# Packed attention and two float32 MLPs on one core: seven small-tile groups a batch in place of twelve, and the first output weights kept as one float32 part until the second stage

## The chip, the core and the metric

The kernel runs on one core of one Trainium2 chip. The core has five engines that run side by side, each through its own list of instructions in order: TensorE (PE in the profile, with its weight loads as PEld), VectorE (DVE), ScalarE (ACT), GpSimd (POOL) and SyncE (SP), which here issues every DMA. They wait for each other by semaphores. The metric is the device time of one execution in microseconds (us), and lower is better.

## The reference

Eight batches of eight heads with 576 tokens are attended in two steps (32 packing queries over all keys, then all queries over the 32 packed rows). The result goes through two MLPs. All inputs are float32, and the weights come to the kernel as float64 words.

```python
def sm_attn(qq, kk, vv):
    s = scale * np.matmul(qq, kk.transpose(0, 1, 3, 2))
    s = s - np.max(s, axis=-1, keepdims=True)
    a = np.exp(s)
    a = a / (np.sum(a, axis=-1, keepdims=True) + 1e-09)
    return np.matmul(a, vv)
p_packed = sm_attn(p, k, v)
out = sm_attn(q, p_packed, p_packed)
x = out.transpose(0, 2, 1, 3).reshape(8 * 576, 512)
h = x @ w_in;  x = np.maximum(0.01 * h, h) @ w_out               # first MLP, 512 -> 2048 -> 512
h = x @ w_in2; return (h * (1 / (1 + np.exp(-1.702 * h)))) @ w_out2
```

## The kernel before

The program has four stages, one after the other. TensorE is fed in all of them with float32 numbers split in a high part (`fp32r`) and a low rest, so that one product is three matmuls (high by high, high by low, low by high).

**Stage 1, attention and the first half of the first MLP** (about the first 354 us). It runs over the batches `b`; each batch has 32 steps `n`, and each step is one call of `l1`: six matmuls of 128x288 into one of three PSUM banks, and a leaky ReLU on ACT (L343), which writes a tile `g`. Four steps fill one `g` tile, which goes to DRAM by SP. After step `n` of batch `b` the agenda is played for step `32*b + n`: `at(step, ...)` puts work there, and `pieces(piece, steps)` spreads the parts of a generator over steps. So the table of step numbers in the middle of the function sets the order on every engine. What is spread is the attention of batch `b+1`: `s1` (scores of the packing queries, softmax numerators `e`), `packed` (transposes `t` of `e`, the product `pp` with the values, its transpose, the packed rows `ppk`), `s2` for two halves of the tokens (scores, softmax, the split `a`), and `prod_m` for four quarters `c` of the hidden units (`ppk` by `w1`, split in `m`). Quarter `c` of `m` is needed from step `8*c` on. `s1`, `pp`, `s2` and `prod_m` are float32 matmuls on parts of the array, 64x32 or 128x32 each, called small-tile groups here; they stand between runs of `l1` matmuls. They write PSUM tiles with the tag `aux`, of which there are five.

Beside it stand the weights of the output product. `combine` takes a 128x512 piece of `w_out1` (sixteen in all), makes float32 of the float64 words (ACT L121 and L122, DVE L125 and L128, POOL L129), forms seven Strassen-like combinations on DVE, splits them in a high and a low part (ACT L155, DVE L157) and stores both in DRAM (`wo1c`). The words are loaded 8 steps before their use.

**Stage 2** computes `y = g w_out1` with a seven-product scheme in six blocks of 768 tokens. A product has 8 steps of six matmuls of 128x384 each (L660). `high` (ACT L496) and `split` (DVE L107) prepare the moving operand a few steps ahead, and `weights` loads the combination `COMBO[p]` in two pieces a product: both parts for `wo1`, one float32 part for `wo2`, which is split by `half` on ACT and DVE. The first five pieces (`EARLY`) are loaded in stage 1, the other nine in the first block of stage 2. **Stage 3** is the first half of the second MLP, **stage 4** its second half, which uses the same `weights`, `prepare` and `evacuate` as stage 2, with `wo2`.

In the diff, `px` is a pool of SBUF that lives until step 24 of the last batch; at that point the loads of the first raw operands of stage 2 (`br`, twelve DMAs) are issued by SP.

Of the kernel before, what the change touches and what calls it, by code (L numbers as in the profile page):

```python
# [46 lines left out]
def packed_attention_moe_moe_kernel(tc, qT, kT, vm, vt, pT, w_in1, w_out1, w_in2, w_out2, out):  # L47
# [8 lines left out]
    wi2c, wo2c = (tc.dram_tile([NJ, P, 7, 256], F32, name=f"{n}_scratch") for n in ("wi2", "wo2"))  # L56
    wo1c = tc.dram_tile([NJ, P, 2, 7, 256], F32, name="wo1_scratch")
# [22 lines left out]
    with ExitStack() as ctx:  # L80
# [51 lines left out]
        def combine(name, source, scratch):  # L132


            conv = pools["conv"]
# [5 lines left out]
            b = conv.tile([P, 8, P], F32, tag="b", name=f"b_{name}")  # L141
            v = conv.tile([P, 4 * P], F32, tag="v", name=f"v_{name}")
# [6 lines left out]
            if scratch is not wo1c:  # L149
                yield  # L150
                nc.sync.dma_start(place(name, scratch), b[:, 1:8])
# [57 lines left out]
        def after(load, b):  # L209
            if b < B:  # L210
                load(b)
# [39 lines left out]
        def packed(b):  # L251

            e, r = e1.pop(b)
            et = px.tile([P, 2, 5, P], F32, tag="et", name=f"et_{b}")
            rest = aux(f"tr_{b}")
            for par in range(2):
                t = aux(f"t1_{b}_{par}")
                for k in range(4):
                    nc.tensor.transpose(t[:, P * k:P * k + P], e[:, par, P * k:P * k + P], ident)
                nc.tensor.transpose(rest[:64, P * par:P * par + P], e[:, par, 512:576], ident)  # L260
                yield
                nc.scalar.copy(et[:, par, 0:4, :], t.rearrange("p (k n) -> p k n", k=4))
# [3 lines left out]
            o = px.tile([P, 2, D], F32, tag="o", name=f"o_{b}")  # L266
            for par in range(2):
                t = aux(f"pp_{b}_{par}")
                for k in range(5):
                    n = P if k < 4 else 64  # L270
                    for i in range(4):
                        c0 = D * (2 * (i % 2) + par)
                        nc.tensor.matmul(t[32 * i:32 * i + 32, :D], lhsT=et[:n, par, k, 32 * i:32 * i + 32],
                                         rhs=v[:n, i // 2, k, c0:c0 + D], start=(k == 0), stop=(k == 4))
                if par and b:
                    after(load_v, b + 1)
                yield
                nc.vector.tensor_scalar(o[:, par, :], t[:, :D], r[:, par:par + 1], None, op0=ALU.mult)
# [114 lines left out]
        run(pk, 4)  # L393
# [22 lines left out]
        for b in range(B):  # L416
            s = 32 * b
            if b + 1 < B:
                if b == 0:
                    first, second = (3, 4, 5, 5, 6, 7), (9, 9, 10, 10, 11, 12, 12, 13)  # L420
                    third, fourth = range(14, 22), range(16, 24)
                else:
                    first, second = (-3, -2, -2, 0, 1, 2), range(5, 13)
                    third, fourth = ([k + i for k in (0, 1, 2, 4, 5, 7, 10, 11)] for i in (13, 17))
                for piece, when in ((s1(b + 1), first), (packed(b + 1), second), (s2(b + 1, 0), third),
                                    (s2(b + 1, 1), fourth), (prod_m(b + 1, 0), range(26, 30))):
                    pieces(piece, [s + k for k in when])
            if b:
                for c in range(1, 4):
                    pieces(prod_m(b, c), [s + 8 * c - 6 + k for k in range(4)])  # L430
# [7 lines left out]
        def weights(first, halves, i, fq, home, scratch, nm):  # L438
# [17 lines left out]
            if scratch is wo1c:  # L456
                return
# [365 lines left out]
```

## Time and the profile before

| what | value |
|---|---|
| time, median of 3 runs (lowest, highest) | 1442.76 us (1441.86, 1443.36) |
| span of the profiled execution | 1443.2 us; no other time stands beside it |
| instructions | 26603 |
| PE busy, PEld busy | 97%, 91% of the span |
| DVE, ACT, POOL busy | 76%, 54%, 7% of the span |
| mean granted TensorE clock | 0.987 of full speed |
| DMA | 317.36 MB, mean 220 GB/s |

The profiled execution has no time of its own beside its span, and the span lies within the three runs, so that sums made against the span hold for the median with 0.4 us taken off. A busy PE is not a PE at its peak: where it stands between two kinds of work, or runs at the lower clock, it is still shown as busy. So the starts of its runs of matmuls, one after another, are read in the timeline.

### The profile page before, as it was taken

Reading aid. Unit: us, or ns where it says so; the run is one execution under the profiler, and the core shown is the slowest. Engines: PE = TensorE matmul, PEld = TensorE weight load, DVE = VectorE, ACT = ScalarE, POOL = GpSimd, SP = SyncE. Lnnn points to the kernel's source line nnn. Section 1 sums busy time; section 2 is a strip of 40 time slices with the busy share of each in tenths; the row PEclk is TensorE's granted clock in tenths of the full one; section 3 lists DMA queues with packets and bytes.
Section 4 is the critical chain, followed back from the end, with each engine's and each line's share of the span. In section 5 each row is a group of like instructions: output and inputs, shape, how many; then the busy total and the mean of one; then the engine's idle time right before and its main releaser. Section 6 shows DMA issues by size and latency. Waiting matters only on the chain. (4 is left out here: it accounts for less than half of the span.)

```text
span 1443.2 us, 26603 instructions
## 1 busy us (share of the span) xinstructions
PE 1395.0 (97%) x10400; PEld 1317.6 (91%) x10400; DVE 1089.9 (76%) x1690; ACT 784.8 (54%) x1413; POOL 95.4 (7%) x71
## 2 busy tenths in 40 slices
PE   5899999999999999999999999999999999999998
PEld 3577777778999999999999999999999999999998
DVE  5757777761879989888978788887559877677775
ACT  4656666665445545554566666666546444444443
POOL 2301011000001111110000001000000000000000
PEclk7999999999999999999999999999999999999999
DMA  9669998969985674664367868777667443515421
GB/s 357 215 231 335 314 318 289 335 211 336 355 295 163 219 242 123 218 219 133 119 219 252 276 231 273 236 259 248 214 231 239 168 142 121 176 56 165 152 68 45
DMA packets 228765, 317.36 MB, mean 220 GB/s; under 512 B 12576, under 2 KB 188704, under 8 KB 228640
## 3 DMA queue, kind: packets, MB, share of 16 engines
q1 hardware_dynamic: 228640, 315.67, 65.8%
q8 instruction: 81, 1.33, 0.4%
q14 instruction: 44, 0.36, 0.1%
HBM read 191.89 MB, written 123.73 MB: 219 GB/s over the span
## 5 line engine op out<-in xcount | busy, mean ns | idle before, releaser
L694 PE MATMUL h<-ya,wj 128*128 128x384 f32 x2016 | 356.3, 338 | 3.7 <-DVE ya L107 2.2
L694 PEld LDWEIGHTS h<-ya,wj 128*128 128x128 f32 x2016 | 353.2, 189 | 6.7 <-DVE ya L107 3.0
L338 PEld LDWEIGHTS h<-a,m 128*128 128x128 f32 x1536 | 211.7, 191 | 57.1 <-ACT g L343 27.0
L338 PE MATMUL h<-a,m 128*128 128x288 f32 x1536 | 234.9, 305 | 13.8 <-ACT a L315 6.5
L496 ACT CAST da<-dr 128x768 fp32r<-128x768 f32 x168 | 140.2, 836 | 171.3 <-PE sum L773 155.1
L773 PE MATMUL sum<-wo,da 128*128 128x256 f32 x1944 | 230.4, 280 | 0.0
L660 PE MATMUL y<-ba,wo 128*128 128x384 f32 x1296 | 227.7, 336 | 2.2 <-DVE ba L107 2.2
L773 PEld LDWEIGHTS sum<-wo,da 128*128 128x128 f32 x1944 | 229.8, 188 | 0.0
L660 PEld LDWEIGHTS y<-ba,wo 128*128 128x128 f32 x1296 | 224.5, 188 | 4.5 <-DVE ba L107 4.5
L496 ACT CAST ba<-br 128x768 fp32r<-128x768 f32 x168 | 140.6, 837 | 156.7 <-PE y L660 127.5
L107 DVE TENSOR_TENSOR da<-dr,da 128x768 fp32r<-128x768 f32 x168 | 160.5, 956 | 75.4 <-ACT da L496 74.4
L107 DVE TENSOR_TENSOR ba<-br,ba 128x768 fp32r<-128x768 f32 x168 | 172.2, 1028 | 41.6 <-ACT ba L496 41.4
L343 ACT ACTIVATE g<-h 128x288 f32<-128x288 f32 x256 | 105.2, 417 | 96.0 <-PE h L338 93.9
L773 PE MATMUL sum<-wo_early,da 128*128 128x256 f32 x1080 | 132.1, 285 | 2.4 <-ACT da L496 1.9
L773 PEld LDWEIGHTS sum<-wo_early,da 128*128 128x128 f32 x1080 | 131.2, 192 | 2.9 <-ACT da L496 2.2
L660 PE MATMUL y<-ba,wo_early 128*128 128x384 f32 x720 | 129.4, 340 | 3.7 <-ACT ba L496 2.7
L660 PEld LDWEIGHTS y<-ba,wo_early 128*128 128x128 f32 x720 | 125.7, 190 | 6.7 <-DVE ba L107 3.4
L327 DVE TENSOR_TENSOR m<-m,m 128x512 fp32r<-128x512 f32 x64 | 43.0, 683 | 49.8 <-ACT m L325 49.3
L129 POOL TENSOR_TENSOR b_wo<-v_wo,b_wo 128x512 int32<-128x512 int32 x32 | 42.3, 1322 | 519.9 <-DVE v_wo L128 414.9
L687 ACT ACTIVATE g<-cc 128x384 f32<-128x384 f32 x96 | 50.3, 524 | 30.8 <-DVE cc L710 26.3
L107 DVE TENSOR_TENSOR wj<-wjs,wj 128x512 fp32r<-128x512 f32 x92 | 58.0, 644 | 9.5 <-ACT wj L634 9.5
L702 DVE TENSOR_TENSOR uv<-uv,h 128x384 f32<-128x384 f32 x48 | 26.5, 552 | 47.0 <-PE h L694 37.6
(115 smaller groups left out, 1336.7 us busy)
## 6 DMA issues: line engine op xcount, KB each, us to landing
g_scratch<-g SPq DMA_DIRECT2D x64, 576.0 KB, 5.3
br<-g_scratch SPq DMA_DIRECT2D x96, 384.0 KB, 6.6
g_scratch<-g SPq DMA_DIRECT2D x96, 384.0 KB, 5.2
dr<-g_scratch SPq DMA_DIRECT2D x96, 384.0 KB, 5.0
wjs<-wi_scratch SPq DMA_DIRECT2D x23, 896.0 KB, 5.7
wo_scratch<-hl_wo SPq DMA_DIRECT2D x32, 448.0 KB, 5.9
wo<-wo_scratch SPq DMA_DIRECT2D x27, 512.0 KB, 9.3
k<-in_kT_dram SPq DMA_DIRECT2D x16, 576.0 KB, 6.7
```

Source lines behind the costliest of these rows:

```text
L107: at(step + 1, lambda: nc.vector.tensor_sub(*rest))
L129: nc.gpsimd.tensor_tensor(d, v.bitcast(I32), d, op=ALU.add)
L327: nc.vector.tensor_sub(m[:, 1, par, :], t[par], m[:, 0, par, :].bitcast(F32))
L338: nc.tensor.matmul(t[:, :TH], lhsT=m[:, ws, par, o:o + P], rhs=a[:, xs, par, :], start=(k == 0), stop=(k == 5))
L343: nc.scalar.activation(g1t[g][:, f % 2, hf * TH:hf * TH + TH], t[:, :TH], AF.Prelu, alpha=0.01)
L496: nc.scalar.copy(t[:, 0], src)
L660: nc.tensor.matmul(acc[BANK[p]][:, c, :HB], lhsT=w[:, ws, P * c:P * c + P], rhs=x[:, xs, :], start=(p in OPENS and f + m == 0), stop=(f == ...
L687: nc.scalar.activation(g[f][:, HB * i:HB * i + HB], src, AF.Gelu_apprx_sigmoid)
L694: nc.tensor.matmul(b, lhsT=w[:, ws, c, P * kk:P * kk + P], rhs=x[:, xs, kk, :], start=(p in OPENS and kk + s == 0), stop=(kk + s == 3), sk ...
L702: nc.vector.tensor_add(v, v, b)
L773: nc.tensor.matmul(b, lhsT=x[:, xs, P * c:P * c + P], rhs=w[:, ws, :], start=(p in OPENS and f == 0 and m == 0 and c != 1), stop=(f == NJ ...
```

## The change

Four things are changed. First, `combine` no longer splits the combinations of `w_out1`: they are stored as one float32 part of half the size, and `weights` loads one part and splits it by `half`, in stage 1 for the five early pieces and in stage 2 for the other nine, as for `w_out2`. Second, the words of `w_out1` are loaded 14 steps ahead of their use, alternately into tiles of `conv` and of `px`. Third, `packed` issues its ten transposes together, and its products `pp` for both head parities together, into one PSUM tile. Fourth, the table of steps is another one: the second half of `packed`, and the quarters 1 and 2 of `prod_m`, start at the same step, so do the two halves of `s2`, and so do quarter 0 of the next batch and quarter 3 of this one.

```diff
-    wo1c = tc.dram_tile([NJ, P, 2, 7, 256], F32, name="wo1_scratch")
+    wi2c, wo1c, wo2c = (tc.dram_tile([NJ, P, 7, 256], F32, name=f"{n}_scratch") for n in ("wi2", "wo1", "wo2"))
...
-            conv = pools["conv"]
+            conv = pools["px" if "px" in pools and name.endswith("1") else "conv"]
...
-            h = pools["px"].tile([P, 2, 7, P], F32R, tag="hl", name=f"hl_{name}")
-            nc.scalar.copy(h[:, 0], b[:, 1:8])
-            yield
-            nc.vector.tensor_sub(h[:, 1], b[:, 1:8], h[:, 0].bitcast(F32))
-            yield
-            for x in range(2):
-                nc.sync.dma_start(place(name, scratch)[:, x], h[:, x].bitcast(F32))
+            yield
+            nc.sync.dma_start(place(name, scratch), b[:, 1:8])
...
+            t = [aux(f"t1_{b}_{par}") for par in range(2)]
             rest = aux(f"tr_{b}")
             for par in range(2):
-                t = aux(f"t1_{b}_{par}")
                 for k in range(4):
-                    nc.tensor.transpose(t[:, P * k:P * k + P], e[:, par, P * k:P * k + P], ident)
+                    nc.tensor.transpose(t[par][:, P * k:P * k + P], e[:, par, P * k:P * k + P], ident)
+            for par in range(2):
                 nc.tensor.transpose(rest[:64, P * par:P * par + P], e[:, par, 512:576], ident)
-                yield
-                nc.scalar.copy(et[:, par, 0:4, :], t.rearrange("p (k n) -> p k n", k=4))
+            yield
+            for par in range(2):
+                nc.scalar.copy(et[:, par, 0:4, :], t[par].rearrange("p (k n) -> p k n", k=4))
...
-            for par in range(2):
-                t = aux(f"pp_{b}_{par}")
+            t = aux(f"pp_{b}")
+            for par in range(2):
...
-                    first, second = (-3, -2, -2, 0, 1, 2), range(5, 13)
-                    third, fourth = ([k + i for k in (0, 1, 2, 4, 5, 7, 10, 11)] for i in (13, 17))
...
-                    pieces(prod_m(b, c), [s + 8 * c - 6 + k for k in range(4)])
-        combined("wo1", range(30, 30 + 16 * 11, 11), 8)
...
+                first, second = range(-5, 1), (1, 2, 4, 5, 6, 7)
+                third, fourth, fifth = (9, 10, 11, 12, 13, 14, 16, 17), (9, 10, 12, 13, 16, 20, 22, 23), (15, 23, 24, 25)
...
+            for c, when in ((1, (4, 5, 6, 7)), (2, (4, 6, 7, 8)), (3, (15, 17, 18, 19))):
+                pieces(prod_m(b, c), [32 * b + k for k in when])
+        slots = [32 * b + k for b in range(1, B - 1) for k in (3, 18, 26) if k != 26 or b < 5]
...
-            if scratch is wo1c:
-                return
```

On PE, batch 3 (the first number behind a name is left out by the print, so `h_3_4_0` is batch 3, hidden block 4, token half 0, and `m_2_0` is quarter 2, parity 0) has before, from step 8 to step 12:

```order
L338 MATMUL h_3_4_0_2197<-a_3_0_1891,m_1_2134 128x288 x6
L273 MATMUL pp_0_2207<-v_1698,et_2159 32x64 x20
L338 MATMUL h_3_4_1_2232<-a_3_1_1948,m_1_2134 128x288 x6
L273 MATMUL pp_1_2241<-v_1698,et_2159 32x64 x20
L338 MATMUL h_3_5_0_2268<-a_3_0_1891,m_1_2134 128x288 x6
L218 MATMUL m_2_0_2277<-w_87,ppk_1750 32x512
L218 MATMUL m_2_1_2278<-w_87,ppk_1750 32x512
...
L338 MATMUL h_3_5_1_2289<-a_3_1_1948,m_1_2134 128x288 x6
L281 MATMUL t_4_2298<-ident,o_2206 128x128
L338 MATMUL h_3_6_0_2306<-a_3_0_1891,m_1_2134 128x288 x6
```

The changed program has, from step 4 to step 8 of the same batch (each kind of `m` row stands four times, alternating):

```order
L330 MATMUL h_3_2_0_2124<-a_3_0_1807,m_0_1938 128x288 x6
L264 MATMUL pp_2134<-v_1623,et_2086 32x64 x40
L207 MATMUL m_1_0_2180<-w_87,ppk_1690 32x512
L207 MATMUL m_1_1_2181<-w_87,ppk_1690 32x512
...
L207 MATMUL m_2_0_2190<-w_87,ppk_1690 32x512
L207 MATMUL m_2_1_2191<-w_87,ppk_1690 32x512
...
L330 MATMUL h_3_2_1_2205<-a_3_1_1900,m_0_1938 128x288 x6
L330 MATMUL h_3_3_0_2219<-a_3_0_1807,m_0_1938 128x288 x6
L273 MATMUL t_4_2227<-ident,o_2133 128x128
L330 MATMUL h_3_3_1_2233<-a_3_1_1900,m_0_1938 128x288 x6
L330 MATMUL h_3_4_0_2249<-a_3_0_1807,m_1_2215 128x288 x6
```

So four groups that had runs of `l1` between them now stand together, and quarter 1, first used by `h_3_4_0`, is made four steps before that use, where it had six.

On DVE, the low part of quarter 0 for batch 4 (`m_0_2556`) stands before behind these rows, ahead of the maxima of `s1` for batch 5:

```order
L308 TENSOR_TENSOR wf_1_2414<-wf_1_2414,s2s_1_2481 128x576
L317 TENSOR_TENSOR a_4_0_2455<-a_0_2454,a_4_0_2455 128x576
L313 STREAM_TRANSPOSE a_1_2510<-wf_1_2414 128x288 x2
...
L148 TENSOR_TENSOR b_wo_3_1_2441<-b_wo_3_1_2441 128x128
L157 TENSOR_TENSOR hl_wo_3_1_2544<-b_wo_3_1_2441,hl_wo_3_1_2544 128x896
L317 TENSOR_TENSOR a_4_1_2511<-a_1_2510,a_4_1_2511 128x576
L327 TENSOR_TENSOR m_0_2556<-m_0_0_2534,m_0_2556 128x512
L327 TENSOR_TENSOR m_0_2556<-m_0_1_2535,m_0_2556 128x512
L239 TENSOR_REDUCE mx_2615<-s_5_0_0_2582 128x1
```

In the changed program the same place reads:

```order
L127 SCALAR_TENSOR_TENSOR v_wo_3_1_2428<-v_wo_3_1_2428,raw_wo_3_1_2201 128x512
...
L144 TENSOR_TENSOR b_wo_3_1_2427<-b_wo_3_1_2427 128x128
L309 TENSOR_TENSOR a_4_1_2452<-a_1_2451,a_4_1_2452 128x576
L146 TENSOR_TENSOR b_wo_3_1_2427<-b_wo_3_1_2427 128x128
L147 TENSOR_TENSOR b_wo_3_1_2427<-b_wo_3_1_2427 128x128
L319 TENSOR_TENSOR m_0_2490<-m_0_0_2371,m_0_2490 128x512
L319 TENSOR_TENSOR m_0_2490<-m_0_1_2372,m_0_2490 128x512
L124 TENSOR_SCALAR raw_wo_4_0_2332<-raw_wo_4_0_2332 128x512
L228 TENSOR_REDUCE mx_2571<-s_5_0_0_2536 128x1
```

The 128x896 row `hl_wo` is gone from DVE, and most of the work of `s2` for batch 4 (`wf`, `a`) has moved up, away from quarter 0.

## Rows read from the trace of the kernel before

**Rows 1.** The page, part 1: busy time, share of the span, instructions.

```profile
PE 1395.0 (97%) x10400; PEld 1317.6 (91%) x10400; DVE 1089.9 (76%) x1690; ACT 784.8 (54%) x1413; POOL 95.4 (7%) x71
```

**Rows 2.** Windows cut at the starts of `s1`: length, busy by engine, clock, DMA share, GB/s.

```profile
85.99:124.06 38.07, 37.34 (x412) 29.94 (x411) 24.84 (x56) 24.47 (x62) 2.56 (x2) 1.00 0.88 293
...
244.69:283.49 38.80, 37.88 (x413) 30.10 (x412) 28.46 (x64) 26.82 (x65) 4.23 (x3) 1.00 0.99 327
283.49:319.80 36.31, 34.31 (x378) 27.43 (x377) 25.32 (x56) 23.92 (x59) 2.58 (x2) 1.00 0.68 217
```

**Rows 3.** Timeline of PE, one batch of stage 1: start, length, work, count.

```profile
85.99 1.20 PE L218 MATMUL s<-k,p 64*32 64x288 f32 x32
87.12 4.27 PE L338 MATMUL h<-a,m 128*128 128x288 f32 x30
91.32 1.09 PE L218 MATMUL m<-w,ppk 64*32 64x512 f32 x16
92.34 2.66 PE L338 MATMUL h<-a,m 128*128 128x288 f32 x18
94.83 0.60 PE L259 MATMUL t<-ident,e 128*128 128x128 f32 x4
...
95.30 1.04 PE L338 MATMUL h<-a,m 128*128 128x288 f32 x6
...
98.41 0.90 PE L273 MATMUL pp<-v,et 128*32 128x64 f32 x40
99.23 1.06 PE L338 MATMUL h<-a,m 128*128 128x288 f32 x6
100.22 0.90 PE L273 MATMUL pp<-v,et 128*32 128x64 f32 x40
...
105.75 0.72 PE L218 MATMUL s<-q,ppk 64*32 64x288 f32 x16
106.39 3.45 PE L338 MATMUL h<-a,m 128*128 128x288 f32 x24
```

**Rows 4.** Timeline of PE at the longest stall of stage 1.

```profile
204.47 1.21 PE L218 MATMUL s<-k,p 64*32 64x288 f32 x14 [2.24 <-DVE m L327]
205.61 6.56 PE L338 MATMUL h<-a,m 128*128 128x288 f32 x30
```

**Rows 5.** Window just behind that stall, columns as in rows 2.

```profile
206.00:210.00 4.00, 4.00 (x18) 4.00 (x18) 2.29 (x7) 1.85 (x4) 0.00 (x0) 0.50 1.00 296
```

**Rows 6.** Groups of ACT and DVE, 85 to 320: busy, mean ns, idle before.

```profile
L343 ACT ACTIVATE g<-h 128x288 f32<-128x288 f32 x191 | 78.7, 417 | 68.2 <-PE h L338 66.2 <-DMA k<-in_kT_dram 1.0 <-DMA wo_scratch<-hl_wo 0.4
L325 ACT CAST m<-m 128x512 fp32r<-128x512 f32 x48 | 28.4, 592 | 0.0
L155 ACT CAST hl_wo<-b_wo 128x896 fp32r<-128x896 f32 x16 | 15.1, 945 | 8.9 <-DVE b_wo L148 8.6 <-issue 0.3
...
L327 DVE TENSOR_TENSOR m<-m,m 128x512 fp32r<-128x512 f32 x48 | 32.1, 682 | 26.2 <-ACT m L325 25.8
L157 DVE TENSOR_TENSOR hl_wo<-b_wo,hl_wo 128x896 fp32r<-128x896 f32 x16 | 17.3, 1080 | 6.7 <-ACT hl_wo L155 5.4 <-DMA raw_wo<-in_w_out_dram 1.1
```

**Rows 7.** Timeline of SP, ACT and PE where stage 2 starts.

```profile
348.83 10.84 SPq L473 DMA_DIRECT2D br<-g_scratch  x12
...
356.15 0.83 ACT L496 CAST ba<-br 128x768 fp32r<-128x768 f32 x1 [1.41 <-DMA br<-g_scratch]
...
357.04 0.44 PE L660 MATMUL y<-ba,wo_early 128*128 128x384 f32 x1 [2.74 <-ACT ba L496]
```

**Rows 8.** Groups of DVE, 1086 to 1138: the weight splits of stage 4.

```profile
L107 DVE TENSOR_TENSOR wo<-wo 128x512 fp32r<-128x512 f32 x18 | 12.0, 682 | 0.0
```

**Rows 9.** Window in the same block, columns as in rows 2.

```profile
1117.00:1127.00 10.00, 10.00 (x87) 10.00 (x87) 10.00 (x14) 7.45 (x12) 0.00 (x0) 1.00 0.59 173
```

**Rows 10.** Timeline of PE: two waits of `pp` in the first batch.

```profile
21.30 1.15 PE L273 MATMUL pp<-v,et 64*32 64x64 f32 x48 [1.99 <-DVE et L263]
...
61.37 0.32 PE L273 MATMUL pp<-v,et 64*32 64x64 f32 x8 [1.94 <-DVE et L263]
```

More of the change, by code (lines that the diff above doesn't have):

```diff
@@ L140, in combine @@
             yield
[L141 to L142 removed]
+            b = conv.tile([P, 8, P], F32, tag="cb", name=f"b_{name}")
+            v = conv.tile([P, 4 * P], F32, tag="cv", name=f"v_{name}")
             yield from to_f32(b[:, 0:4].rearrange("p i w -> p (i w)"), raw.rearrange("p i (w t) -> p (i w) t", t=2), v, True)
@@ L272, in packed @@
                         c0 = D * (2 * (i % 2) + par)
-                        nc.tensor.matmul(t[32 * i:32 * i + 32, :D], lhsT=et[:n, par, k, 32 * i:32 * i + 32],
+                        nc.tensor.matmul(t[32 * i:32 * i + 32, D * par:D * par + D], lhsT=et[:n, par, k, 32 * i:32 * i + 32],
                                          rhs=v[:n, i // 2, k, c0:c0 + D], start=(k == 0), stop=(k == 4))
[L275 to L278, printed above, removed]
+            if b:
+                after(load_v, b + 1)
+            yield
+            for par in range(2):
+                nc.vector.tensor_scalar(o[:, par, :], t[:, D * par:D * par + D], r[:, par:par + 1], None, op0=ALU.mult)
             yield
@@ L392, in packed_attention_moe_moe_kernel @@
         run(w1p[3], 2)
-        run(pk, 4)
+        run(pk, 2)
         run(w1p[4], 2)
@@ L415, in packed_attention_moe_moe_kernel @@
             pieces(prod_m(0, c), when)
-        for b in range(B):
+        for b in range(B - 1):
             s = 32 * b
[L418 to L422, printed above, removed]
-                    first, second = (-3, -2, -2, 0, 1, 2), range(5, 13)
-                    third, fourth = ([k + i for k in (0, 1, 2, 4, 5, 7, 10, 11)] for i in (13, 17))
[L425 to L429, printed above, removed]
-                    pieces(prod_m(b, c), [s + 8 * c - 6 + k for k in range(4)])
-        combined("wo1", range(30, 30 + 16 * 11, 11), 8)
+            if b == 0:
+                first, second = (3, 4, 5, 5, 6, 7), (9, 10, 11, 12, 13, 13)
+                third, fourth, fifth = range(14, 22), range(16, 24), range(26, 30)
+            else:
+                first, second = range(-5, 1), (1, 2, 4, 5, 6, 7)
+                third, fourth, fifth = (9, 10, 11, 12, 13, 14, 16, 17), (9, 10, 12, 13, 16, 20, 22, 23), (15, 23, 24, 25)
+            for piece, when in ((s1(b + 1), first), (packed(b + 1), second), (s2(b + 1, 0), third),
+                                (s2(b + 1, 1), fourth), (prod_m(b + 1, 0), fifth)):
+                pieces(piece, [s + k for k in when])
+        for b in range(1, B):
+            for c, when in ((1, (4, 5, 6, 7)), (2, (4, 6, 7, 8)), (3, (15, 17, 18, 19))):
+                pieces(prod_m(b, c), [32 * b + k for k in when])
+        slots = [32 * b + k for b in range(1, B - 1) for k in (3, 18, 26) if k != 26 or b < 5]
+        for n, s in enumerate(slots):
+            j, u = divmod(n, 2)
+            pieces(combine(f"wo1_{j}_{u}", w_out1_v[:, :, j, :, u, :], wo1c), (s - 14, *(s + k for k in (0, 1, 2, 4, 5, 6))))
         steps = [(blk, p, f) for blk in range(NBK) for p in PRODUCTS for f in range(NJ)]
@@ L449, in load @@
                 wt[p, fq] = t
[L450 to L454 removed]
+                nc.sync.dma_start(t[:, 1].bitcast(F32), scratch[4 * fq:4 * fq + 4, :, COMBO[p], :].rearrange("f p w -> p f w"))
             at(first, load)
[L456 to L457 removed]
             def half(k):
```

8 lines of the change are left out of this document (removed).

## The prediction

> **What bounds the kernel now.** The page comes first: PE is busy for 97% of the span [rows 1], so a gain must come from PE's own time. Busy does not mean at full rate, and the reader should look at how PE's work follows on. Windows cut at the starts of `s1` give the length of a batch period in stage 1: 38.07 us for the first of five, 38.80 for the last, and 197.5 for the five together, as they run from 85.99 to 283.49 [rows 2].
>
> The timeline of PE gives the price of everything in such a period [rows 3]. Thirty `l1` matmuls take 4.20 us from start to start of what follows (87.12 to 91.32), six take 0.99 (99.23 to 100.22): 0.134 each, and 0.19 at the end of a run that a small-tile group follows. In front of transposes the end costs less: 18 take 2.49 (92.34 to 94.83), 0.09 more than 18 times 0.134. A group of `m` takes 1.02 (91.32 to 92.34), `pp` 0.82, `t` with its rest 0.47 (94.83 to 95.30). A group of `s2` takes 0.64 (105.75 to 106.39), and the two groups of `s1`, which stand together, 1.13 (85.99 to 87.12): 0.16 less than twice 0.64. So a group that stands alone pays 0.19 on entering and 0.16 inside, 0.35 together, which a second group beside it does not pay.
>
> Added up, a period without any waiting is 192 matmuls (25.7), four `m` (4.1), two `s2` (1.3), two `pp` (1.6), `s1` (1.1), nine run ends (1.7) and the transposes (1.1): 36.7 us. The five periods thus lose 197.5 - 183.5 = 14.0 us. The piece from 283.49 to 319.80 is a period short of one `m` and 18 matmuls (3.6 us): it should take 33.1 and takes 36.31 [rows 2], 3.2 more. That is **17.2 us of stalls** in stage 1.
>
> The longest shows their kind: PE stands 2.24 us in `s1` because the low part of quarter 0 on DVE (L327), which must free a PSUM tile, is late; after it 30 matmuls take 6.56 instead of 4.27 [rows 3, 4], because the granted clock has fallen to 0.50, which is 1.2 of 2.4 GHz [rows 5]. DVE was late as its queue holds, ahead of quarter 0, the 1.08 us split of `hl_wo`, which itself waits for ACT's 0.95 us copy [rows 6]. Bursts on ACT and DVE around PE's needs are thus the second limit, though each engine has room on average.
>
> **The change, part by part.**
>
> *Groups put together.* In batches 1 to 6, two `pp` and quarters 1 and 2 become one island (three joins), two halves of `s2` one (one join), quarters 0 and 3 one (one join): five joins of 0.35, 1.75 us a batch, 10.5 for six. The last batch joins quarters 1 and 2, the first its two `pp`: 0.7 more. Joining the transposes is worth 0.09 at most, and I count nothing. Together **11.2 us**. One join is not in the rows: from `pp` (128x32) to `m` (64x32) the shape of the tiles changes. It may save nothing or the full 0.35; I take 0.35, as for `s1`, whose border also changes weights at every matmul, and keep 0 for the range (2.1 us less).
>
> *The split of `w_out1` leaves stage 1.* Sixteen copies of 0.95 on ACT and sixteen subtractions of 1.08 on DVE go [rows 6], 32 us of work off the two engines whose lateness makes the stalls. Five early pieces come back as ten copies and ten subtractions of 128x512 (0.68 each on DVE [rows 8]), all but one piece's in the last batch, where no attention is left to prepare; they cost nothing there, and if they did, a copy of 0.6 ahead of a leaky ReLU is still covered by the three banks of `h`, two steps of 0.8.
>
> *The new table.* Quarter 3's low part is asked for at steps 18 and 19 instead of 20 and 21, for a use at step 24, and quarter 0's low part has less in front of it on DVE, as the order shows. The tightest place is now quarter 1: made at step 4, used at step 8. With zero at the end of its island: the next run ends at 0.80, ACT's ReLU (0.42) at 1.22, the first copy (0.59) at 1.81; the next ReLU at 2.23, the second copy at 2.82; DVE's second subtraction (0.68) at 3.50 [rows 6]. PE passes three runs and a transpose (2.5) and wants that part with the last of the fourth run's matmuls, at 3.2. So a wait of 0.3 a batch is left by mean durations. The five `aux` tiles are all in use after this island; the next to want four of them is `s2` at step 9, and by the same walk quarter 2's last subtraction is over by then, but closely. I therefore allow 0.5 us of new waits a batch, 3.0 for six, and of the 17.2 count **14.2 us** as won. The bounds are 17.2 and nothing.
>
> *Words 14 steps ahead, half the bytes stored and loaded.* A wait of ACT for words would end; in rows 6 DMAs appear behind only some 2.5 us of idle time on both engines, so it is worth nothing by itself.
>
> *The start.* Two waits of PE for DVE's copy `et` of 1.99 and 1.94 us stand in batch 0's and batch 1's `pp` [rows 10]. For the first, both copies and DVE's now stand ahead of the next conversion of `w_in1`: the copy is no longer late, but the same conversions stand in front of `s2`'s DVE work next, so I take **1.0** of 1.99 (bounds 0 and 1.99). For the second, `pp` comes one step later (0.8 us of matmuls in between), and its wait shrinks by **0.8** (0 to 1.94).
>
> *The start of stage 2.* The first `ba` copy waits for a DMA, and PE for the copy, 2.74 us [rows 7]. The load was issued at 348.83 and used at 356.15: 7.3 us, behind 1 MB of early weights, which now are 0.5 MB, and behind a queue that each batch step now fills less. At the 327 GB/s of rows 2 half a MB is 1.6 us, and the emptier queue adds to it. I take **2.0 us** (0 to 2.74, and up to 2.3 more if the clock then stays up, by what it cost in rows 4).
>
> *The splits that come to stage 2.* Nine pieces give 18 copies and 18 subtractions, 12 us of DVE [rows 8], into the first block. Stage 4 does precisely that with the same steps: there DVE is full, 10.00 of 10, and PE too, with 87 matmuls in 10 us and no gap [rows 9]. Low parts are asked for three steps ahead, which is 3.1 us with nine of those matmuls a step. I cost it at **nothing**; what hides it is that lead. Without it at most the 12 us themselves would be PE's.
>
> **Sum:** 11.2 + 14.2 + 1.0 + 0.8 + 2.0 = 29.2 us, from the span of 1443.2 to 1414.0; the median lies 0.4 below the span, and I leave it at **1414**.
>
> **The rivals.**
>
> *The stalls stay.* ACT and DVE still carry two thirds of their work in bursts; the walk above has 0.3 us of lack at one place and others may follow. If half of the 17.2 stay, the time is 1443.2 - 8.6 - 15.0 = 1419.6, if all, 1428. For it: waits move rather than vanish. Against it: 32 us of the late work is gone.
>
> *DMA becomes the bound of stage 1.* In the last of the five periods DMA is busy at 0.99 with 327 GB/s [rows 2], 12.7 MB in 38.8 us. With 1.3 MB less (some 2.9 stores of 0.46 MB a period), 11.4 MB in my 34.9 us is again 327 GB/s, with nothing to spare; batches 1 to 4 have three pieces each, slightly more than before. If the period stays at 36.5 in six batches, that is 10 us: 1424. Against it: loads are 14 or 32 steps ahead and four `g` tiles cover 16 steps; hardly any wait above ends with a DMA.
>
> *The clock falls behind the long islands.* The joined island of 3.2 us holds no 128x128 work. If the granted clock fell behind it as it did in rows 5, 2.3 us would go in each of six batches [rows 4]: 14 us, 1428; with the joined quarters 0 and 3 too, 28 us, 1442. Against it: the clock is 1.00 in the periods of rows 2, with twelve islands each, and the run of six behind the transposes takes 1.04 against 1.06 [rows 3]. The Trainium skill, TensorE: Matmul & The Clock Gate, Part 4: PE-mode transpose, says that transposes do not count as busy the way matmuls do, which would speak for a fall behind the joined transposes as well; no row here shows one.
>
> *Stage 2 pays for the splits.* If a third of the 12 us came through, with a fall of the clock (2.3), that is 6.3: 1420. Against it stands stage 4 [rows 9].
>
> *Slower: quarter 1 comes too late at step 8.* ACT's two copies stand behind two ReLUs that wait for runs issued after the island. If ACT or DVE were 2 us behind there, PE would stand 2.24 or more, and the clock would fall: 4.5 a batch, 27 in six, 1441, no change. It decides for slower, 1446 and up, from a lateness of 3.1 us on, which with 2.3 for the clock makes 5.4 a batch against a gain of 29.2. The walk says 0.3.
>
> **How the numbers follow.** My forecast (1408 to 1420) has a chance of 0.60; stalls that stay 0.14; DMA 0.10; the clock 0.05, of it 0.02 near no change; stage 2 0.03; quarter 1 late 0.08, of it 0.05 far enough for slower. The range goes from 1407 (all stalls gone, 3.0 more, and the start of stage 2 at its bound) to 1428 (all stalls stay, or one fall of the clock a batch). About 0.2%, 2.9 us, is what a measurement of this kernel can tell from no change: faster 0.90, same 0.05, slower 0.05.
>
> **What would show it.** Right: periods from `s1` to `s1` near 35.4 us at clock 1.00; one island with `pp` and two `m` of about 3.2 us; no wait of PE for L327's successor above 0.5 us; the first `y` matmul closer behind the last `h` than 2.7 us; stage 2's first block with no PE gap and DVE full. Wrong: a half clock behind the long island, a wait at the first run that uses quarter 1, ACT waiting for stores of `g`, or PE waiting for a `wo` subtraction.

## The result and the profile after

The changed kernel takes **1422.5 us** (median of 4 runs, 1420.43 to 1423.68); the kernel before, run beside it, 1442.54 (4 runs, 1441.86 to 1443.36). The ratio is 0.9858 [0.9841, 0.9875]. That is faster, as predicted, and inside the range, but 8.5 us above the predicted 1414: of 29.2 us counted, 20.0 came.

The profiled execution of the changed kernel took 1420.43 us with a span of 1418.7. In every run that gives both numbers, time is span plus 1.7 to 1.8. The page of before, with its span of 1443.2, thus belongs to an execution of about 1444.9, which is 2.4 above that kernel's median, and the page of after to one 2.1 below its own. Between the two traces the difference is 24.5 us, 4.5 more than between the medians; I keep the two apart.

First the page's part 1, which answers to [rows 1], and then windows of the changed kernel cut at the starts of `s1`, with the columns of [rows 2].

```profile
PE 1378.1 (97%) x10400; PEld 1312.9 (93%) x10400; DVE 1089.7 (77%) x1702; ACT 781.0 (55%) x1425; POOL 94.6 (7%) x71
```

```profile
82.36:119.49 37.13, 36.26 (x412) 30.31 (x411) 24.15 (x55) 23.86 (x62) 2.57 (x2) 1.00 0.77 266
119.49:155.36 35.87, 35.61 (x413) 30.25 (x412) 25.42 (x61) 23.79 (x62) 3.87 (x3) 1.00 0.96 320
```

PE is as busy as before, and only the periods tell: they have become equal. Four of the five take 35.87, where before they took 37.92 to 43.61; the five together take 180.6 instead of 197.5 [rows 2].

The timeline of PE over one period answers to [rows 3].

```profile
119.49 1.20 PE L207 MATMUL s<-k,p 64*32 64x288 f32 x32
...
129.11 1.67 PE L264 MATMUL pp<-v,et 128*32 128x64 f32 x76
...
130.66 1.90 PE L207 MATMUL m<-w,ppk 64*32 64x512 f32 x28
132.48 1.86 PE L330 MATMUL h<-a,m 128*128 128x288 f32 x12
...
134.21 3.04 PE L330 MATMUL h<-a,m 128*128 128x288 f32 x18
137.17 1.20 PE L207 MATMUL s<-q,ppk 64*32 64x288 f32 x32
...
143.30 1.95 PE L207 MATMUL m<-w,ppk 64*32 64x512 f32 x32
145.18 10.25 PE L330 MATMUL h<-a,m 128*128 128x288 f32 x72
```

The islands stand as the table orders: `pp` with two `m` from 129.11 to 132.48 (3.37 us), two halves of `s2` in 1.13, quarters 0 and 3 in 1.88. Counted in the timelines, the runs of `l1` are broken at twelve places a period before (three of them transposes) and at six now: the title's seven leaves out that the transposes `t` were joined too. No wait is marked. But lengths can be compared with counts: 18 matmuls at 0.134 with the 0.19 at a run's end are 2.60, and the run from 134.21 takes 2.96; 72 take 9.79 where nothing holds them up (e6_tuned below), and the run from 145.18, up to the next `s1` at 155.36, takes 10.18. **0.36 and 0.39 us beyond the count are hidden inside runs** in each period, and no row names them as waits; that they are waits is what the runs below look for.

At the start of stage 2 the same stretch as in [rows 7] reads so (SP, ACT, PE), and the windows around it so:

```profile
326.52 8.62 SPq L461 DMA_DIRECT2D br<-g_scratch  x12
...
332.48 2.29 ACT L484 CAST ba<-br 128x768 fp32r<-128x768 f32 x3
...
333.36 0.44 PE L648 MATMUL y<-ba,wo_early 128*128 128x384 f32 x1 [1.22 <-ACT ba L484]
334.35 0.44 PE L648 MATMUL y<-ba,wo_early 128*128 128x384 f32 x1 [0.55 <-DVE ba L106]
```

```profile
332.00:336.00 4.00, 2.23 (x12) 1.84 (x11) 1.93 (x3) 2.60 (x4) 0.00 (x0) 1.00 1.06 387
336.00:340.00 4.00, 4.00 (x25) 4.00 (x24) 4.00 (x5) 1.68 (x2) 0.00 (x0) 1.00 1.06 373
```

The 2.74 us of PE have become 1.22, no DMA stands ahead of ACT's copy, and the clock stays at 1.00 in this trace.

Where the 24.5 us of the traces arose, cut at the first `h` (35.16 before, 33.52 after), the start of the first of these periods (85.99, 82.36) and the second `y` matmul (358.03, 334.35): 1.64 ahead of the first `h`, 1.99 up to the first period, 20.05 from there to `y`, 0.82 in all that follows (1085.17 against 1084.35).

### The profile page after: what moved, and what is told of

Same layout as the page of the kernel before. It is cut to its first block, busy times and chain, and to the rows that moved or that the text cites. A ratio compares the mean times of both kernels' runs of the same rounds, so it can differ in the third digit from the quotient of the medians.

```text
span 1418.7 us, 26535 instructions
## 1 busy us (share of the span) xinstructions
PE 1378.1 (97%) x10400; PEld 1312.9 (93%) x10400; DVE 1089.7 (77%) x1702; ACT 781.0 (55%) x1425; POOL 94.6 (7%) x71
## 5 line engine op out<-in xcount | busy, mean ns | idle before, releaser
L330 PEld LDWEIGHTS h<-a,m 128*128 128x128 f32 x1536 | 208.6, 189 | 39.1 <-issue 15.1
L330 PE MATMUL h<-a,m 128*128 128x288 f32 x1536 | 223.1, 301 | 11.7 <-ACT a L307 6.5
```

What stands on the lines that cost most here:

```text
L330: nc.tensor.matmul(t[:, :TH], lhsT=m[:, ws, par, o:o + P], rhs=a[:, xs, par, :], start=(k == 0), stop=(k == 5))
```

## The experiments

All ratios are to the kernel before, run beside it on the same chip. "Period" is the distance of two starts of `s1` in the middle of stage 1.

| run | us, median | ratio [95%] | period |
|---|---|---|---|
| r_after | 1423.47 | 0.9858 [0.9843, 0.9873] | 35.86 |
| e2_split_back | 1423.75 | 0.9871 [0.9844, 0.9897] | 35.91 |
| e3_old_table | 1439.1 | 0.9973 [0.9962, 0.9983] | 37.76 to 40.57 |
| e4_unjoined | 1425.83 | 0.9877 [0.9861, 0.9894] | 36.43 |
| e5_words8 | 1424.21 | 0.9871 [0.985, 0.9893] | 35.87, 36.05 |
| e1_late_half | 1421.53 | 0.9846 [0.9832, 0.9861] | 35.85 |
| e6_tuned | 1421.15 | 0.9848 [0.9832, 0.9864] | 35.88 |
| e7_steps | 1423.38 | 0.9862 [0.9843, 0.9881] | 36.13 |
| e8_leads | 1445.19 | 1.0017 [1.0007, 1.0027] | 39.4 to 41.4 |
| e9_late | 1418.92 | 0.9834 [0.9814, 0.9854] | 35.65 |
| e10_words | 1429.99 | 0.9913 [0.9897, 0.993] | 37.45 |
| e11_both | 1420.15 | 0.9838 [0.9824, 0.9851] | 36.0 |

**The changed kernel again** (r_after), no edit.

> The changed kernel once more, to compare the next three with on the same chip. In its first profile stage 2 lost some 2.5 us in its first block: a weight load waits for the landing of the last g store, ACT stands 3.07 us for the weights in front of the first split, and PE then waits 0.71 and 0.51 us for the moving operand. Theory A (the late weights): its executions spread over 3 us, because in some of them that wait is longer and the clock falls; a second profile shows the same wait of ACT of 2 to 5 us at the same place. Rival B (DVE is simply over-full with the splits): the wait for DMA is not there again, and PE waits spread over the whole block.

It gave 1423.47, and neither theory fits: ACT waits 1.06 us for the same load, where it was 3.07, and PE's waits of 0.71 and 0.51 are not there. Instead the granted clock fell right behind the first `y`, with waits of PE equal to those of the first trace (1.22 and 0.55):

```profile
334.94:338.94 4.00, 4.00 (x14) 4.00 (x15) 2.97 (x4) 0.77 (x2) 0.00 (x0) 0.58 1.07 379
```

From the second `y` on this trace is 1.31 us longer than the first (1085.66 against 1084.35), and 0.6 up to there: so much do two executions of one program differ, in the first block of stage 2 too, which the change touches.

**Split or table?** Two runs take the change apart. The first puts the old split's work back under the new table, with the words loaded 8 steps ahead again:

```diff
+            if scratch is wo1c:
+                h = raw.rearrange("p i w -> p (i w)")[:, :896].bitcast(F32R).rearrange("p (a w) -> p a w", a=7)
+                nc.scalar.copy(h, b[:, 1:8])
+                yield
+                nc.vector.tensor_sub(h, b[:, 1:8], h.bitcast(F32))
```

> The changed kernel with the two operations of the old split put back into each of w_out1's sixteen pieces, ACT's copy and DVE's subtraction of 128x896 (0.95 and 1.08 us), at the old place in the sequence; their result is dropped, so no byte more is stored or loaded, and nothing else moves. Words are loaded 8 steps ahead, as before. Theory A, my prediction's: the bursts of the split made DVE late for PE, so the stalls come back; the 17.2 us stood in six batches, and if half of them return the time is 1432, periods near 37.3. Theory B: the new table, which asks for each quarter earlier and puts fewer but larger groups on PE, ended the stalls; then periods stay at 35.9 within 0.3 and the time at 1423 to 1425.

The other takes the split out of the kernel before and leaves its table:

```diff
...
-            h = pools["px"].tile([P, 2, 7, P], F32R, tag="hl", name=f"hl_{name}")
-            nc.scalar.copy(h[:, 0], b[:, 1:8])
-            yield
-            nc.vector.tensor_sub(h[:, 1], b[:, 1:8], h[:, 0].bitcast(F32))
...
+            yield
+            nc.sync.dma_start(place(name, scratch), b[:, 1:8])
...
```

> The kernel before with the split of w_out1 alone taken out (one part stored and loaded, halves made in y): the table of steps and the twelve small-tile groups a batch are those of before. No join can pay here (11.2 us of the prediction). Theory A, the split's bursts made the stalls: 14.2 us of stalls and the 3 us at the start of stage 2 go, 1443.3 - 17.2 = 1426, periods near 36.7 as added up without waiting. Theory B, the table made them: the stalls stay, and only the start of stage 2 gains, 1440; periods of 38.1 to 38.8 stay within 0.3.

DVE's group in e2_split_back from 85 to 320 (busy, mean ns, idle before) shows that the work is back, and a window of one of its periods that it costs nothing there:

```profile
L154 DVE TENSOR_TENSOR raw_wo<-b_wo,raw_wo 128x896 fp32r<-128x896 f32 x16 | 17.1, 1072 | 2.5 <-ACT raw_wo L152 2.5
```

```profile
156.35:192.26 35.91, 35.72 (x413) 30.30 (x412) 27.74 (x64) 26.39 (x65) 3.88 (x3) 1.00 0.92 318
```

ACT and DVE are busy for 2.6 and 2.3 us more in that period, which is 0.04 longer. So under the new table theory A fell: 32 us of work back on the two engines, and no stall with it in the periods. (In the last batch PE waits 1.06 and 1.14 us for leaky ReLUs, at 301.04 and 332.64, where r_after has one wait of 0.47; by the medians no difference is shown.) In e3_old_table the work is gone too, and the five periods sum to 192.9: less than the 197.5 of before, but 9.4 above the prediction's 183.5 without any waiting. Two of its windows, and the waits of PE in 85 to 320 (total, times, longest):

```profile
199.77:237.53 37.76, 37.66 (x412) 30.02 (x412) 25.18 (x61) 24.37 (x62) 4.25 (x3) 1.00 0.89 297
237.53:278.10 40.57, 38.03 (x412) 30.15 (x411) 26.18 (x61) 24.57 (x62) 4.34 (x3) 1.00 0.88 287
```

```profile
PE h L327 <- ACT g L332: 3.4, 2, 2.4
PE h L327 <- DVE m L316: 1.2, 2, 0.6
```

PE's waits for DVE's low parts, 5.8 us in the same stretch of before, have fallen to 1.2, and the granted clock no longer falls in a period; but 3.4 us of waits for leaky ReLUs have come. In front of both of these ReLUs ACT stands at a conversion of words:

```profile
191.14 0.67 ACT L120 ACTIVATE b_wo<-raw_wo 128x512 int32<-128x512 uint32 x1 [0.91 <-DMA wo_scratch<-b_wo]
...
271.15 0.67 ACT L120 ACTIVATE b_wo<-raw_wo 128x512 int32<-128x512 uint32 x1 [2.35 <-issue]
```

This run stores the combinations from the tile that the next words are converted into, and it has one such tile where the changed kernel alternates between two. The first wait is for that store; for the second the trace names nothing. So the run is no clean removal of the split. It gained 3.9 us (0.0027 of the time); without its two new waits, by an estimate from this one trace, the periods would come to 189.5, so that under the old table some 8 of the 14.0 us of stalls went with the split and 6 did not. Under the new table the split costs nothing that could be measured. By the time alone theory B's 1440 was nearly met.

**What in the table?** One rival was the lead: the old table makes each low part three steps ahead of its first use.

```diff
-                                    (s2(b + 1, 1), fourth), (prod_m(b + 1, 0), range(26, 30))):
+                                    (s2(b + 1, 1), fourth), (prod_m(b + 1, 0), range(24, 28))):
...
-                    pieces(prod_m(b, c), [s + 8 * c - 6 + k for k in range(4)])
+                    pieces(prod_m(b, c), [s + 8 * c - 8 + k for k in range(4)])
```

> The kernel before, with its split and its twelve small-tile groups a batch, and each quarter of batches 1 to 6 asked for two steps earlier, so its low part is made five steps ahead of its first use instead of three (except quarter 0 and 1 of the first batches' edges); nothing else. Theory B1, the old table's short leads made the stalls: the waits of PE for that subtraction, 5.8 us in the trace of before, and the falls of the clock behind them go, and the time comes to 1430 to 1435. Theory B2, the number of groups and where they stand made them: the time stays at 1442.8 within 2 us.

1445.19, slower by 0.17%. The waits moved, as PE's in 85 to 320 show:

```profile
PE h L338 <- ACT g L343: 4.8, 3, 3.1
PE h L338 <- DVE m L327: 2.3, 4, 1.3
```

The longest are now for leaky ReLUs, and in front of the longest ACT stands at the split's copy, as it does 3.09 us ahead of quarter 0 at the longest stall of before. The first row is of e8_leads, the second of before:

```profile
164.40 0.94 ACT L155 CAST hl_wo<-b_wo 128x896 fp32r<-128x896 f32 x1 [3.24 <-issue]
```

```profile
201.08 0.94 ACT L155 CAST hl_wo<-b_wo 128x896 fp32r<-128x896 f32 x1 [3.09 <-DVE b_wo L148]
```

So with the split in place longer leads do not help; longer leads without the split were not tried. The opposite edit, on the changed kernel:

```diff
-                ... (15, 23, 24, 25)
+                ... (15, 25, 26, 27)
-            ... (3, (15, 17, 18, 19))):
+            ... (3, (15, 19, 20, 21))):
```

> The changed kernel with its islands as they are, and the copies and subtractions of quarter 3 made two steps later (last one at step 21, three steps ahead of its first use, the lead of the kernel before) and those of quarter 0 two steps later too (27, five ahead). Theory B1, leads: PE waits for quarter 3 in some or all batches as it did before, periods of 36.4 and more, 1426 to 1430. Theory B2: leads of three steps are enough with fewer groups, periods stay at 35.9 within 0.2 and the time at 1423 within 1.5; the run of 72 matmuls may even lose its 0.39 us of delay, since the copies then no longer stand with the words' conversions on ACT, so 1421 is its lower end.

Theory B1 fell here too. With quarter 3's lead back at three steps the period is 0.22 shorter, and the time the best of all: four runs of 1418.79 to 1419.5, against 1420.43 to 1423.9 in eight of after. (Its interval overlaps that of after, so by how much it is better is not settled.)

One number of the new table no run took back by itself: the steps of the words. They came every 11 steps, so at other places in each period, and come at steps 3, 18 and 26 now. That such places matter is seen in e10_words below, where moving them alone made a period 1.3 us longer.

**Groups apart again.** Quarter 0 and one half of `s2` are moved out of their islands by one step:

```diff
-                third, fourth, fifth = (...), (9, 10, 12, 13, 16, 20, 22, 23), (15, 23, 24, 25)
+                third, fourth, fifth = (...), (10, 11, 12, 13, 16, 20, 22, 23), (16, 23, 24, 25)
```

> The changed kernel with two of the five joins of a batch undone: the second half of s2 one step later (step 10) and quarter 0 one step later (step 16). Theory A (a group alone pays 0.35 us): a period from s1 to s1 goes from 35.87 to 36.6 us, 0.70 more, and six batches make the kernel 4 us slower than the changed one. Rival B (the joins are worth nothing, all gain is of stalls that went): the period stays at 35.9, and the time within 1 us.

The period grew by 0.57, in every batch alike, and the time by 2.4 us (there the intervals overlap; the periods show it): a join is worth 0.28, a little under the 0.35 of my prediction. The lone groups cost 0.65 and 1.02 as in [rows 3]; some 0.1 comes back in the run of matmuls behind quarter 0.

**The hidden waits.** Four runs try to take away the 0.36 and 0.39 us, all with the late weight half of e1_late_half (below) in them. The first asks for quarter 1's low part earlier, and starts words' second piece at step 19 instead of 18:

```diff
-            for c, when in ((1, (4, 5, 6, 7)), ...
+            for c, when in ((1, (4, 5, 5, 6)), ...
-        ... for k in (3, 18, 26) if k != 26 or b < 5]
+        ... for k in (3, 19, 26) if k != 26 or b < 5]
```

> The changed kernel with three small moves: the late split of the run before; quarter 1's second copy and both subtractions one step earlier (steps 5, 5 and 6 in place of 5, 6 and 7); the second words of w_out1 in a batch converted from step 19 in place of 18. Theory A: the two hidden delays of a period, some 0.36 us in the matmuls of steps 7 to 9 (PE wants quarter 1) and 0.39 us in steps 16 to 27 (ACT has two copies and two conversions in a row), go; the period falls from 35.87 to 35.1 to 35.3 us, and with the stage 2 wait the kernel is 4 to 7 us faster than the changed one. Rival B (these delays are the price of the islands themselves): the period stays at 35.8 or more, and only stage 2 gains, 1 to 3 us.

The run of 72 lost its delay (217.56 to 227.35, 9.79); that it was a leaky ReLU behind words' conversions on ACT fits e7_steps below, where the delay is back and half of it marked as such a wait. At step 8 the wait grew until it could be seen, 0.54 us. DVE's and PE's timeline there:

```profile
206.49 0.69 DVE L319 TENSOR_TENSOR m<-m,m 128x512 fp32r<-128x512 f32 x1 [3.12 <-ACT m L317]
207.10 0.68 DVE L127 SCALAR_TENSOR_TENSOR v_wo<-v_wo,raw_wo 128x512 uint32<-128x512 uint32 x1
207.70 1.28 DVE L319 TENSOR_TENSOR m<-m,m 128x512 fp32r<-128x512 f32 x2
```

```profile
208.44 1.19 PE L330 MATMUL h<-a,m 128*128 128x288 f32 x7 [0.54 <-DVE m L319]
```

An operation on words (L127) had slipped between quarter 1's two subtractions. The next run starts words' first piece at step 6 instead of 3:

> The changed kernel with three numbers of the table moved: the third and fourth step of quarter 1 come at 5 and 6 instead of 6 and 7, words' pieces start at steps 6, 19 and 26 instead of 3, 18 and 26 (so no operation on words stands between quarter 1's two subtractions on DVE, and the later piece is not in a row with quarter 3's copies on ACT), and the first late weight piece of stage 2 is split at steps 15 and 16. If the 0.36 and 0.39 us by which the runs of matmuls in steps 7 to 9 and 16 to 27 are longer than their count are lateness of quarter 1's subtraction and of the leaky ReLU, the period falls from 35.87 to about 35.15, and the time by 3 to 4 us to 1419. If they are a property of the matmuls after an island, the period stays at 35.87 and the time at 1421.5 as with the late half alone.

The subtractions came in time, and the wait went one engine on, to ACT's copy for `s2`, behind the conversions of the words; 0.18 to 0.20 us of the delay in the run of 72 is now marked as a wait for a leaky ReLU. ACT and PE, 0.34 us in each batch:

```profile
208.67 0.71 ACT L120 ACTIVATE b_wo<-raw_wo 128x512 int32<-128x512 uint32 x1
209.24 0.71 ACT L121 ACTIVATE v_wo<-raw_wo 128x512 f32<-128x512 f32 x1
209.79 0.45 ACT L335 ACTIVATE g<-h 128x288 f32<-128x288 f32 x1
210.08 0.32 ACT L276 COPY ppk<-t 128x128 f32<-128x128 f32 x1
```

```profile
210.45 1.20 PE L207 MATMUL s<-q,ppk 64*32 64x288 f32 x32 [0.34 <-ACT ppk L276]
```

So the pieces were put where ACT stood idle, at steps 8, 15 and 26 (the only difference from e7_steps):

> As the run e7_steps, with the words' pieces at steps 8, 15 and 26: their conversions then come to ACT behind the island of step 9 and that of step 15, where ACT stood idle for 1.7 and 2.2 us in the changed kernel's trace. In e7_steps PE waited 0.34 us a batch for ACT's copy ahead of s2 and 0.20 for a leaky ReLU, both behind these conversions; if that was the cause, period 36.13 - 0.54 = 35.6 or a little less, and 1421 to 1422 with the late half in; if quarter 3's run loses its 0.39 us too, 35.2 and 1419. Rival: the words' operations on DVE push the softmax back, quarter 3's subtraction comes late, and the period stays at 35.9 or rises to 36.3.

Worse than e7_steps by 6.6 us; the rival named there is what happened, and more of it. ACT's waits in 80 to 345, and one place in the timeline:

```profile
ACT a L307 <- DVE a L305: 18.4, 12, 2.1
```

```profile
193.62 0.67 ACT L307 CAST a<-a 128x576 fp32r<-128x576 f32 x1 [2.12 <-DVE a L305]
194.20 0.40 ACT L335 ACTIVATE g<-h 128x288 f32<-128x288 f32 x1
...
194.65 1.85 PE L330 MATMUL h<-a,m 128*128 128x288 f32 x12 [1.21 <-ACT g L335]
```

Here the reader sees the mechanism whole. The words push the softmax on DVE back; ACT, which works in order, stands 2.12 us at the softmax's copy; the leaky ReLU behind it could run but does not; all banks of `h` fill, and PE stands 1.21 us. ACT's idle time was no free room: it ended where DVE's chain let it.

**The late weight half.** The changed kernel with the first late piece of `wo1` split three steps later:

```diff
-                weights(..., (8 * i - 6 + 2 * fq, 8 * i - 5 + 2 * fq), i, fq, home(n), scratch, nm)
+                d = 3 if n == EARLY and nm == "wo1" else 0
+                weights(..., (8 * i - 6 + 2 * fq + d, 8 * i - 5 + 2 * fq + d), i, fq, home(n), scratch, nm)
```

> The changed kernel, with the split of the first late weight piece of stage 2 asked for three steps later (steps 15 and 16 in place of 12 and 13); PE uses it at step 20. Theory A: ACT no longer stands in front of it, PE's waits in the first block of stage 2 fall below 0.5 us in all, the time falls by 1 to 3 us against the changed kernel on the same chip, and its executions spread less. Rival B (DVE over-full): the same number of subtractions in the same block, so PE waits as before, within 0.5 us.

ACT's wait of 3.07 us for that load, at 348.84 in after, is gone; one of PE's two waits remained (0.60). But r_after, which has the load as it was, has neither of the two, and the intervals of e1_late_half and r_after overlap: at most 2 us, not shown to be anything.

**Words 8 steps ahead.** `(s - 14, ...)` becomes `(s - 8, ...)` in the list of words' steps.

> The changed kernel with w_out1's words loaded 8 steps ahead instead of 14, nothing else. My prediction's term for this is nothing: 1423 within 1 us. Rival: ACT waits for words and the leaky ReLU stands behind it; 8 steps are some 8.6 us, and a load that lands later than that in a period with DMA at 0.9 would stop ACT, at 0.5 us or more in each of 14 pieces, so 1426 to 1430.

1424.21, within a microsecond of r_after: nothing that could be measured, as forecast. ACT does wait for words four times (5.3 us in 80 to 345), and PE once behind it, 0.31 us.

**Both good edits together**: e9_late, quarter 1 at (4, 5, 5, 6), the words' third step one later, and the late half.

> The run e9_late with two things more: quarter 1's two subtractions back to back on DVE (its third and fourth step at 5 and 6, and the words' shift-and-or one step later, so that it stands behind both of them, where in e6_tuned it stood between them), and the late weight half of e1_late_half. No operation on ACT is moved into another place ahead of a leaky ReLU or of the copy for s2, which is what cost e7_steps and e10_words their time. If quarter 1's subtraction alone makes the run of 18 matmuls take 2.96 us instead of 2.60, the period falls from 35.65 to 35.3 and the time by 2 us to 1417; with something of the late half 1416. If another limit stands behind it, period 35.65 and 1418.9 within 0.7.

1420.15, period 36.0: a miss. The run of 18 came to 2.78 and that of 72 to 9.80, 0.18 better each than in e9_late, and `s1` took 1.88 instead of 1.13, with no wait marked. DVE and PE there:

```profile
227.16 0.29 DVE L146 TENSOR_TENSOR b_wo<-b_wo 128x128 f32<-128x128 f32 x1
...
227.69 1.28 DVE L319 TENSOR_TENSOR m<-m,m 128x512 fp32r<-128x512 f32 x2
```

```profile
227.20 1.95 PE L207 MATMUL s<-k,p 64*32 64x288 f32 x32
```

Quarter 0's subtractions, which free the tiles that `s1` needs, run from 227.69 to 228.97, behind the words' operations that I had moved one step on, and `s1` lasts to 229.15.

## Why the prediction was right, and where its size was off

*Joins, 11.2 us counted.* Shown for two of the five of a batch, a little smaller: 32 joins of 0.28 (e4_unjoined) are 9.1; by the lengths of the islands themselves they are 10.3, since only the one with `pp` fell short, at 3.37 us where I counted 3.22. The border from `pp` to `m`, left open there, saves 0.20 of its 0.35.

***Stalls, 14.2 of 17.2 counted as won: this term failed***, in size, and in cause by half. Of the 20.05 us between the first `s1` and `y`, 31 joins take 8.7 to 9.9 and the start of stage 2 takes 1.52; that leaves **9 us**, in the traces. By the medians, which are 4.5 closer together, it is less, though 1.64 of those 4.5 can be what came ahead of the first `h` (below).

What remained is the 0.75 us a period in two hidden pieces, where I had allowed 0.5 of new waits; 1.28 in the first period's `s1` behind quarter 0's subtraction; and runs in the last batch that are longer than their counts. That stalls hide so could have been read in the trace of before. This is the window and the PE timeline of the one period of before without any marked wait:

```profile
163.16:201.08 37.92, 37.79 (x413) 30.00 (x412) 27.84 (x62) 24.86 (x61) 3.86 (x3) 1.00 1.01 335
```

```profile
163.16 1.99 PE L218 MATMUL s<-k,p 64*32 64x288 f32 x32
165.08 4.25 PE L338 MATMUL h<-a,m 128*128 128x288 f32 x30
...
190.38 7.17 PE L338 MATMUL h<-a,m 128*128 128x288 f32 x48
197.47 1.09 PE L218 MATMUL m<-w,ppk 64*32 64x512 f32 x16
```

`s1` takes 1.92 here instead of 1.13, and 48 matmuls take 7.09 where later ones, from 320.82 to 327.41, take 6.59: 1.3 us, which is all that lies between 37.92 and the sum of pieces, 36.7. The marked waits of PE between 85 and 320 sum to 7.7, and the fall of the clock cost 2.3; so some 7 of the 17.2 were of the hidden kind, in every period, and these I had no reason to count as won: the new table has hidden ones of its own.

The cause was half right. I took the splits of `hl_wo` for it because one stood ahead of the late subtraction [rows 4, 6]. Under the old table that is borne out in part: without the split PE's waits for DVE's low parts fall from 5.8 us to 1.2 and the clock stays up (e3_old_table), and in before and e8_leads ACT stands more than 3 us at the split's copy ahead of the longest stall. But the hidden part stays, every period of e3_old_table being at least 1.06 us above 36.7, and under the new table the same work costs nothing in a period (35.91, e2_split_back). So the table as a whole ended the stalls, with the split or without it. Which of its numbers did, beyond the joins, stays open; the steps of the words are the rival that was not tried.

*The start, 1.0 and 0.8.* 1.64 came ahead of the first `h`, but not for the reason counted: that the 1.0 was met is luck. Rows of before, of after and of e3_old_table:

```profile
17.38 0.60 PE L259 MATMUL t<-ident,e 128*128 128x128 f32 x4
```

```profile
14.97 1.57 PE L248 MATMUL t<-ident,e 128*128 128x128 f32 x8
...
20.02 0.30 PE L273 MATMUL t<-ident,o 128*128 128x128 f32 x1 [1.60 <-DVE o L270]
```

```profile
19.81 1.15 PE L262 MATMUL pp<-v,et 64*32 64x64 f32 x48 [1.99 <-DVE et L252]
...
34.35 0.61 PE L327 MATMUL h<-a,m 128*128 128x288 f32 x1 [7.34 <-ACT a L304]
```

The wait of 1.99 is gone, but the next one, for DVE's `o`, is 1.60 where it was 0.41. From the transposes to the first `h` the changed kernel takes 18.55 us, and before 17.78, as does e8_leads; what it gained lies ahead of the transposes, in work that the change leaves alone. And e3_old_table, which keeps the 1.99, has its first `h` at 34.35, among the runs with the new `packed` (33.52 to 34.42). So the step that failed is that a shorter wait of `pp` would bring the first `h` forward; no run shows that it does. The second wait fell from 1.94 [rows 10] to 0.91: right.

*The start of stage 2, 2.0.* 1.52 came, and the clock did not fall in the trace of after, but it did in r_after. My reason, half a MB less ahead of the load, is not borne out: e8_leads keeps the two-part weights and waits 1.24 there. The 2.74 of [rows 7] may have been one execution's: all other thirteen traces have 1.22 to 1.24.

*Splits in stage 2, nothing.* Near right, though not by the plain sum: from the second `y` to the end it is 1085.17 before, 1084.35 and 1085.66 after, but the clock fell behind the first `y` in before (0.63 from 358 to 362) and in r_after, and not in after. Where it did not fall, e8_leads, without these splits, takes 1083.58, and the nine traces with them 1083.44 to 1085.52, most of them 0.5 to 1.0 more than e8_leads. DVE is full there, and in after PE waits twice, 0.71 at 351.98 and 0.51 at 361.33, where I had expected no gap.

*Words 14 steps ahead, nothing.* Right (e5_words8).

*The base.* The sum was taken from a span and compared with a median as if the two were 0.4 apart; taken from the median it gives 1442.5 - 29.2 = 1413.3. This moved the forecast by 0.7 us only. The range's lower end, added up from its terms, is 1408, not 1407. What weighed more was that one trace, of an execution 2.4 us above the median, priced the stalls.

*The rivals.* "The stalls stay", at half 1419.6, is the one that came nearest. DMA rose to 0.96 with 320 GB/s, and no wait of PE in the five periods ends with a DMA. The clock did not fall behind the long island; windows around the transposes and the island in the changed kernel:

```profile
125.00:129.00 4.00, 4.00 (x34) 3.94 (x32) 0.82 (x4) 2.95 (x11) 0.00 (x0) 1.00 0.99 370
129.00:133.00 4.00, 4.00 (x118) 2.34 (x117) 1.50 (x4) 1.74 (x4) 0.89 (x1) 1.00 1.08 364
```

The rule of the Trainium skill, TensorE: Matmul & The Clock Gate, Part 4: PE-mode transpose, that transposes do not count as busy as matmuls do, led to no fall here: the granted clock is 1.00, the 2.4 GHz level, in both windows. Quarter 1 was late at step 8, by at most 0.36 (0.18 came back in e11_both) against the 0.3 of the walk, far from the 3.1 at which that rival turns to slower.

## What to carry to other kernels

Before counting stalls as winnable, compare the length of each run with its count: a wait that no row names repeats in every period, and a new order brings its own. Between engines that work in order, an operation that is moved into idle time of one costs what stands behind it on all of them; read the queue behind it (e7_steps, e10_words, e11_both each moved one and paid elsewhere). And a work item that stands ahead of a late one may be its cause in that order alone: put it back under the new order and take it out of the old one before it gets the credit, and look whether the run that takes it out brings a wait of its own (e3_old_table).

## What the hardware showed that I had not expected

The clock does not follow from the length of a wait, not even in one program. At the start of stage 2 PE waits 1.22 (once 1.24) and 0.55 us in thirteen traces alike. In the 4 us behind the second wait the granted clock stays at 1.00 in ten of them, the first trace of after among them, and is at 0.57 or 0.58 in three: r_after, which is the same program, e3_old_table and e4_unjoined. Such a fall cost some 1.5 us: 119 matmuls of `y` take 22.41 in r_after and 20.90 in e1_late_half. Nor did e3_old_table's longest wait, 2.40 us up to 272.71, bring a fall, where 2.24 us did in [rows 4, 5]. Windows of e3_old_table behind that wait and at the start of its stage 2:

```profile
273.00:277.00 4.00, 4.00 (x39) 3.00 (x39) 3.04 (x8) 2.02 (x6) 1.76 (x1) 1.00 0.72 229
...
349.00:353.00 4.00, 3.45 (x11) 3.29 (x11) 3.22 (x4) 1.13 (x2) 0.00 (x0) 0.58 1.06 376
```

What makes the difference is not shown. For a learner it means that a term for the clock, priced from one trace, is a chance and not a gain.
